# A copy moved ahead of a root, the last adds begun with the first tile, and the last tile cut at column 320, in a fused attention and gMLP kernel

## Chip, cores, metric

One core of a Trainium2 chip. The metric is the device time of one execution in microseconds; the profile's span is about 1.8 us shorter than it.

## The reference

A layer norm of x [2048, 512]; a dilated local attention on it (32 heads of 16, window 8, dilation 2, with output projection); a gMLP on it (projection to 2 x 688, gelu, layer norm of the second half, a [2048, 2048] product over tokens, gating, output projection); and the sum of x and both branches. Cut to what the change touches:

```python
x  = A_x
xn = layernorm(x)
return x + A_ref(xn, A_wqkv, A_wo) + B_ref(xn, B_w_in, B_w_sp, B_b_sp, B_w_out)

# A_ref: qkv = xn @ wqkv; softmax(q . k over 8 keys, 2 apart) @ v; @ wo
# B_ref: z = gelu(xn @ w_in); z1, z2 = halves; z2 = layernorm(z2)
#        (z1 * (w_sp @ z2 + b_sp)) @ w_out
```

## The kernel before

The tokens are 16 tiles of 128, in four blocks: tile `4 * tb + j` belongs to block j. `t0, i1, i2, i3` are the tiles of blocks 0 to 3. For every tile: statistics on VectorE, one over the root of the variance on ScalarE (`ln_root`), the norm applied on VectorE (`ln_apply`), and a transpose into `xnT`, from which TensorE makes q, k, v and z. A tile is transposed either on TensorE and copied out of PSUM by ScalarE (`tr`, `tr_copy`; for two tiles of block 0 half of the copy is VectorE's), or by a DMA that the SyncE queue issues (`tr_dma`). The engines run in the order in which the code emits instructions; waits come from the data.

```python
def ln_root(sl):
    A.activation(rstd[:, sl], mv[:, sl, 1], ACT.Abs_reciprocal_sqrt, bias=eps_t[:])

def tr_copy(i, pt, c0=0, c1=C):
    A.copy(xnT[:, c0:c1, i * P:(i + 1) * P], pt[:, c0:c1, :])

def tr_dma(i):
    j, tb = i % 4, i // 4
    SP.dma_start_transpose(xnT[:, :, i * P:(i + 1) * P], xall[:, j, tb, :])
...
    # end of the block 1 preparation; tiles 0 and 1 go over TensorE, 2 and 3 by DMA
    tr_dma(i1[2])
    ln_agg(i1[3])
    ln_root(col(i1[3]))
    ln_apply(i1[3])
    tr_dma(i1[3])
    load_x(SP, 3, 0, 4)
    pq3 = qk_tile()
    qk_part(pq3, 0, 3, 0, 4, (0,), kcs=range(2))
    pt = tr(i1[1])
    qk_part(pq3, 0, 3, 0, 4, (0,), kcs=range(2, 4))
    tr_copy(i1[1], pt)
    qk_part(pq3, 0, 3, 0, 4, (1,))
    qk_copy(pqs[2], 0, 2)
    qk_copy(pq3, 0, 3)
    for n in range(4):
        ln_stats(i2[n])
    ln_root(slice(2, 7, 4))
    ln_root(slice(10, 15, 4))
    for i in i2:
        ln_apply(i)
        tr_dma(i)
    for n in range(4):
        ln_stats(i3[n])
    ...                       # q and k of block 1: first from tiles 0 and 1, then from 2 and 3
    ln_root(blk_cols(3))
    qk_copy(pqs[0], 1, 3, 2, 4)
```

Then a fixed order of steps follows (`z j.tb`: z product of a tile; `zg`: its gelu, which frees the PSUM buffer; `q`: q/k product; `p`: products on VectorE). Three PSUM buffers of two banks take turns for z and q.

```python
ORDER = """
z2.0 z1.3 p1.1 z2.2 zg2.0 p0.1 zg1.3 q2.2 zg2.2 ...
... Or3 Oh3.0 Oh3.1 F3.0 F3.1 s3.0 s3.1 end
"""
LASTCUT = 288
```

The end of the program is the output projection of the last group, four tiles of 128 tokens, summed in PSUM. Tiles 0 and 1 share a buffer of two banks, tile 2 has its own, and tile 3 is split by columns over two buffers. Each sum is added to x by VectorE and stored.

```python
def out_half(o, h):                       # Oh: 5 matmuls for each of two tiles
    for tb in (2 * h, 2 * h + 1):
        for part in range(len(tiles["o", o][tb])):
            out_full(o, tb, part)

def last_adds():                          # end
    for tb, part, E in ((2, 0, SP), (3, 0, A), (3, 1, SP)):
        out_add(3, tb, part)
        out_store(3, tb, part, E)
```

Of the kernel before, what the change touches and what calls it, by code (L numbers as in the profile page):

```python
# [10 lines left out]
ALU = mybir.AluOpType  # L11
# [3 lines left out]
P = 128  # L15
# [11 lines left out]
F = 1376  # L27
FH = 688
FHALF = 344
MCH = 7  # L30
# [25 lines left out]
U10 Oh1.1 Fe1.0 U9 T8 Gi14 A43 Fe1.1 A44 T10 X13 A45 G11 s0.2 T9 A46 s0.3 F1.0 A47 A48 G13 F1.1 Gi11 s1.1 Xg13  # L56
U11 U12 Fe1.2 A49 T12 A50 A51 X14 A52 G15 Xg14 Fe1.3 U14 Gi13 F1.3 F1.2 A53 s1.2 T11 A54 T14 A55 O2 Gi15 s1.0
A56 U15 U13 T15 A57 Or2 xr2 Oh2.0 A58 A59 s1.3 Oh2.1 T13 Fe2.0 Fe2.1 xr3 F2.0 O3 Fe2.2 Fe2.3 F2.2 F2.1 s2.0
s2.2 F2.3 s2.1 s2.3 Or3 Oh3.0 Oh3.1 F3.0 F3.1 s3.0 s3.1 end
"""  # L60
NZ1 = 8
LASTCUT = 288


def slot_w(s):
# [4 lines left out]
def kernel(  # L70
# [13 lines left out]
    V = nc.vector  # L84
    A = nc.scalar
    G = nc.gpsimd
    PE = nc.tensor
    SP = nc.sync
# [19 lines left out]
    wout = r_w[:, 4096:4096 + MCH * D].rearrange("p (m n) -> p m n", m=MCH)  # L108
# [19 lines left out]
    uT = r_uz[:, NZ1 * FPAD:].rearrange("p (s m t) -> p s m t", s=2, m=MCH)  # L128
    pr_home = [r_pr[:, 0:8192], r_pr[:, 8192:16384], r_uz[:, (NZ1 + 8) * FPAD - 8192:]]
    pr = [h.rearrange("p (c w b t) -> p c w b t", w=4, c=C, b=TB) for h in pr_home]  # L130
    xl_t = [r_pr[:, n * D:(n + 1) * D] for n in range(4)]
    ol_t = [r_pr[:, (4 + n) * D:(5 + n) * D] for n in range(4)]
# [39 lines left out]
    def load_x(E, j, b0, b1):  # L172
        for tb in range(b0, b1):
            E.dma_start(xall[:, j, tb], xblk[j][:, tb])
# [42 lines left out]
    def ln_agg(i, parts=1):  # L217
        V.bn_aggr(mv[:, i, :], stats[:, i, 0:6 * parts])

    def ln_root(sl):  # L220
        A.activation(rstd[:, sl], mv[:, sl, 1], ACT.Abs_reciprocal_sqrt, bias=eps_t[:])

    def ln_apply(i):
        j, tb = i % 4, i // 4
        V.tensor_scalar(xall[:, j, tb, :], xall[:, j, tb, :], mv[:, i, 0:1], rstd[:, i:i + 1],
                        ALU.subtract, ALU.mult)
# [8 lines left out]
    def tr_copy(i, pt, c0=0, c1=C):  # L235
        A.copy(xnT[:, c0:c1, i * P:(i + 1) * P], pt[:, c0:c1, :])
# [12 lines left out]
# [3 lines that stand above are left out]
# [57 lines left out]
    def qk_part(pq, j, m, b0, b1, ccs=(0, 1), p0=None, kcs=range(C)):  # L309
        sd, c0 = m // 2, 2 * (m % 2)  # L310
        p0 = b0 if p0 is None else p0
        xv = xnT[:].rearrange("p k (b j t) -> p k b j t", b=TB, j=4)
        for cc in ccs:
            for kc in kcs:
                PE.matmul(pq[:, cc, p0 * P:(p0 + b1 - b0) * P], wqk[:, sd, kc, c0 + cc:D:C],  # L315
                          xv[:, kc, b0:b1, j, :], start=(kc == 0), stop=(kc == C - 1))
# [7 lines left out]
    def qk_copy(pq, j, m, b0=0, b1=TB, p0=None):  # L324
        sd, c0 = m // 2, 2 * (m % 2)
        p0 = b0 if p0 is None else p0
        if sd == 0:
            dst = qs[:, j, c0:c0 + 2, b0 * P:b1 * P].rearrange("p c (b t) -> p c b t", b=b1 - b0)
        else:
            dst = ks[:, c0:c0 + 2, HALO:HALO + S].rearrange("p c (b j t) -> p c b j t", b=TB, j=4)[:, :, b0:b1, j, :]  # L330
        cast = A.copy(dst, pq[:, :, p0 * P:(p0 + b1 - b0) * P].rearrange("p c (b t) -> p c b t", b=b1 - b0))  # L331
        if sd == 1:
            for i in k_reads[j]:
                tc.declare_no_dep(cast.ins, i, reason="other token columns of the same rows")
            k_casts[j].append(cast.ins)

    def qk_tile():
        return ps_mm.tile([P, 2, TBS], F32, name="pq", tag="mm")
# [157 lines left out]
    def out_heads(o):  # L496
# [13 lines left out]
        if last:  # L510
            cuts[3] = [(pos[3][:, 0:LASTCUT], slice(0, LASTCUT)), (pb[:, 0, 0:D - LASTCUT], slice(LASTCUT, D))]
        tiles["o", o] = cuts
# [19 lines left out]
    def out_add(o, tb, part=0):  # L532
        pc, cs = tiles["o", o][tb][part]
        if o == 3:
            V.tensor_tensor(ol_t[tb][:, cs], pc, xl_t[tb][:, cs], ALU.add)  # L535
        else:
            V.tensor_tensor(ot_t[tb], ot_t[tb], xr_t[tb], ALU.add)

    def out_store(o, tb, part=0, E=SP):
        i = 4 * tb + ORD[o]  # L540
        pc, cs = tiles["o", o][tb][part]
        E.dma_start(out2[i * P:(i + 1) * P, cs], (ol_t if o == 3 else ot_t)[tb][:, cs])

    def out_full(o, tb, part=0):
        pc, cs = tiles["o", o][tb][part]
        for m in range(MCH - 2):
            PE.matmul(pc, uT[:, o % 2, m, tb * P:(tb + 1) * P], wout[:, m, cs],  # L547
                      start=False, stop=(m == MCH - 3))

    def out_half(o, h):  # L550
        for tb in (2 * h, 2 * h + 1):
            for part in range(len(tiles["o", o][tb])):
                out_full(o, tb, part)

    def last_adds():
# [3 lines that stand above are left out]
# [4 lines left out]
    def blk(j):  # L563
        return [4 * tb + j for tb in range(TB)]

    def col(i):
        return slice(i, i + 1)
# [9 lines left out]
    t0, i1 = blk(0), blk(1)  # L577
# [50 lines left out]
    ln_apply(i1[2])  # L628
    tr_dma(i1[2])
    ln_agg(i1[3])  # L630
    ln_root(col(i1[3]))
    ln_apply(i1[3])
    tr_dma(i1[3])
    load_x(SP, 3, 0, 4)
    pq3 = qk_tile()
    qk_part(pq3, 0, 3, 0, 4, (0,), kcs=range(2))
    pt = tr(i1[1])
    qk_part(pq3, 0, 3, 0, 4, (0,), kcs=range(2, 4))
    tr_copy(i1[1], pt)
    qk_part(pq3, 0, 3, 0, 4, (1,))  # L640
    qk_copy(pqs[2], 0, 2)
    qk_copy(pq3, 0, 3)
# [41 lines left out]
    def halo_zero():  # L684
# [7 lines left out]
             "st": lambda k: st[k](), "N": z2_norm,  # L692
             "M": sm_max, "E": sm_exp, "S": lambda h, k: sm_sum(h, k), "R": sm_norm, "mask": add_mask,
             "G": g_mm, "Gi": g_bias, "U": u_mul, "T": u_tr, "A": lambda k: ap[k](),
             "O": out_heads, "Or": out_rest, "Oh": out_half, "Fe": out_evac, "F": out_add, "s": out_store, "end": last_adds,
             "halo": halo_zero, "wo": load_wo, "late": load_late, "xr": load_xr, "w": load_wsp}
    for tok in ORDER.split():
        name = tok.rstrip("0123456789.")
# [31 lines left out]
```

## Time and profile before

| | before |
|---|---|
| time, 3 runs | 202.38 us (202.26 to 202.41) |
| span of the profiled execution | 200.2 us |
| TensorE busy | 195.9 us, 98% |
| VectorE, ScalarE busy | 92%, 52% |
| transposes of block 1's second tile start | 12.91 us |
| first z load of block 2 | 21.67 us |
| last add ends | 197.83 us |

Busy shares say that TensorE is full; they don't say whether a hole of a tenth of a microsecond can be closed. That is read from single starts in the timeline. In the lines of the profile, PE is TensorE, PEld its weight loads, DVE VectorE, ACT ScalarE and SPq the queue of SyncE; a bracket gives the idle time before a group and what ended it. Two lines beside those that the prediction shows give the stretch that part 1 is about (start, duration, engine, line):

```profile
13.13 4.24 PE L315 MATMUL pq<-xnT,r_w 128*128 128x512 bf16 x30
17.20 1.04 PE L315 MATMUL pa<-xnT,r_w 128*128 128x256 bf16 x8
```

### The profile page before, as it was taken

The numbers are of one execution on the slowest core, as the hardware profiler recorded it, in microseconds if no ns is written. First come the engines' busy times: TensorE is split into PE (matmuls) and PEld (weight loads), VectorE is DVE, ScalarE is ACT, GpSimd is POOL, SyncE is SP. The second block draws the span as 40 slices with busy tenths as digits, with TensorE's granted clock in tenths as the row PEclk, the third lists the DMA queues.
The fourth block names the chain that finished last, engine by engine and source line by source line (L and its number), as shares of the span: only waits on it lengthen the run. The fifth ranks groups of instructions, "written<-read, shape, count | busy, mean of one in ns | idle before, by whom it ended". The sixth has DMA issues, their size and how long they took to land.

```text
span 200.2 us, 4094 instructions
## 1 busy us (share of the span) xinstructions
PE 195.9 (98%) x1691; PEld 124.1 (62%) x1691; DVE 184.5 (92%) x249; ACT 104.0 (52%) x176; POOL 18.5 (9%) x14
## 2 busy tenths in 40 slices
PE   7999999999999999999999999999999999999994
PEld 2869756665566666666656666666544646664562
DVE  5799999999989999999979999999999999999605
ACT  3586987899899986453431523708402230331400
POOL 3000000899400000000000000000000000000000
DMA  5877689940000095524467999199920295219863
GB/s 162 258 248 174 100 96 274 211 79 3 0 0 3 3 177 94 167 65 100 73 139 170 244 225 170 46 219 177 221 58 0 86 227 144 72 37 124 214 208 105
DMA packets 66562, 25.91 MB, mean 129 GB/s; under 512 B 56496, under 2 KB 66288, under 8 KB 66288
## 3 DMA queue, kind: packets, MB, share of 16 engines
q1 hardware_dynamic: 65824, 25.19, 57.8%
q10 hardware_dynamic: 720, 0.47, 0.7%
q8 instruction: 13, 0.21, 0.5%
q14 instruction: 5, 0.04, 0.1%
HBM read 10.13 MB, written 2.10 MB: 61 GB/s over the span
## 4 chain that ended last, share of the span: by engine, by line
PE 95%; DVE 2%; DMA 1%; issue 0%; SPq 0%; ACT 0%
PE pg L464 37%; PE pz L257 19%; PE pq L315 12%; PE pv L425 7%; PE po L547 7%; PE po L517 6%; PE pq L321 2%; DMA r_x<-in_A_x_dram 1%; PE pa L547 1%; PE pl L375 1%; DVE r_pr L535 1%; PE po L526 1%; PE pb L517 1%; PE pa L315 0%; PE pt L232 0%
## 5 line engine op out<-in xcount | busy, mean ns | idle before, releaser
L464 PE MATMUL pg<-z,r_qk 128*128 128x344 bf16 x448 | 66.8, 309 | 0.0
L464 PEld LDWEIGHTS <-r_qk 128*128 128x128 bf16 x448 | 43.8, 98 | 22.0 <-issue 0.4
L439 DVE TENSOR_TENSOR r_pr<-r_x,r_w 128x2048 bf16<-128x2048 bf16 x32 | 38.4, 1219 | 1.3 <-PE pl L375 1.0
L257 PE MATMUL pz<-w_z,xnT 128*128 128x344 bf16 x256 | 39.3, 309 | 0.0
L443 DVE TENSOR_TENSOR r_pr<-r_pr 128x2048 bf16<-128x2048 bf16 x28 | 33.9, 1218 | 0.4
L257 PEld LDWEIGHTS <-xnT 128*128 128x128 bf16 x256 | 24.9, 98 | 13.4 <-issue 0.4
L470 ACT ACTIVATE gs<-pg,b_col 128x688 bf16<-128x688 f32 x16 | 13.2, 833 | 35.4 <-PE pg L464 26.4
L355 DVE TENSOR_TENSOR r_pr<-r_qk 128x2048 bf16<-128x2048 bf16 x24 | 27.8, 1216 | 0.5 <-ACT r_qk L331 0.5
L315 PE MATMUL pq<-xnT,r_w 128*128 128x512 bf16 (+1 forms) x136 | 24.9, 335 | 0.0
L315 PEld LDWEIGHTS <-r_w 128*128 128x128 bf16 x144 | 15.9, 114 | 7.7 <-issue 0.6
L672 POOL CAST b_col<-b 128x16 f32<-128x16 bf16 x1 | 16.4, 16439 | 33.0 <-DMA b<-in_B_b_sp_dram 33.0
L530 ACT CAST r_qk<-po 128x512 bf16<-128x512 f32 x10 | 5.5, 588 | 22.7 <-PE po L547 22.7
L331 ACT CAST r_qk<-pq 128x1024 bf16<-128x1024 f32 (+1 forms) x16 | 15.4, 984 | 2.5 <-PE pq L315 2.4
L306 ACT ACTIVATE r_uz<-pz 128x688 bf16<-128x688 f32 x16 | 11.7, 740 | 6.6 <-PE pz L257 6.5
L517 PE MATMUL po<-r_lg,r_pr 32*128 32x512 bf16 x192 | 14.5, 375 | 0.0
L425 PE MATMUL pv<-xnT,r_w 128*32 128x512 bf16 x256 | 14.2, 379 | 0.0
L547 PEld LDWEIGHTS <-r_uz 128*128 128x128 bf16 x85 | 8.1, 98 | 9.4 <-issue 1.1
L364 DVE TENSOR_TENSOR r_pr<-r_pr 128x4096 bf16<-128x4096 bf16 x6 | 13.7, 2283 | 0.0
L547 PE MATMUL po<-r_w,r_uz 128*128 128x512 bf16 x60 | 13.6, 380 | 0.0
L281 ACT ACTIVATE junk<-z 128x688 bf16<-128x688 bf16 x16 | 12.4, 774 | 0.1
L275 ACT ACTIVATE z<-pz 128x688 bf16<-128x688 f32 x16 | 11.8, 740 | 1.2 <-PE pz L257 1.2
L425 PEld LDWEIGHTS <-r_w 128*32 128x32 bf16 x256 | 9.5, 138 | 4.2
(85 smaller groups left out, 194.6 us busy)
## 6 DMA issues: line engine op xcount, KB each, us to landing
r_lg<-in_A_wo_dram SPq DMA_DIRECT2D x8, 256.0 KB, 4.0
r_x<-in_A_x_dram SPq DMA_DIRECT2D x12, 128.0 KB, 3.2
out_dram<-r_qk SPq DMA_DIRECT2D x12, 128.0 KB, 2.2
r_w<-in_A_wqkv_dram SPq DMA_DIRECT2D x8, 128.0 KB, 3.5
r_qk<-in_A_x_dram SPq DMA_DIRECT2D x8, 128.0 KB, 2.2
w_z<-in_B_w_in_dram SPq DMA_DIRECT2D x4, 172.0 KB, 5.2
w_z<-in_B_w_in_dram SPq DMA_DIRECT2D x1, 688.0 KB, 5.4
r_w<-in_B_w_out_dram SPq DMA_DIRECT2D x1, 640.0 KB, 7.1
```

The source lines that it names most:

```text
L257: PE.matmul(pz[:, hh, 0:FHALF], xnT[:, kc, i * P:(i + 1) * P], wz[:, kc, hh * FHALF:(hh + 1) * FHALF], start=(kc == 0), stop=(kc == C - 1))
L315: PE.matmul(pq[:, cc, p0 * P:(p0 + b1 - b0) * P], wqk[:, sd, kc, c0 + cc:D:C], xv[:, kc, b0:b1, j, :], start=(kc == 0), stop=(kc == C - 1))
L331: cast = A.copy(dst, pq[:, :, p0 * P:(p0 + b1 - b0) * P].rearrange("p c (b t) -> p c b t", b=b1 - b0))
L355: prod = V.tensor_tensor(pr[g % 3][:, c].rearrange("p w b t -> p b w t"), q3.unsqueeze(2).broadcast_to([P, TB, 4, P]), k4, ALU.mult)
L364: V.tensor_tensor(pr[g % 3][:, 0:2], pr[g % 3][:, 0:2], pr[g % 3][:, 2:4], ALU.add)
L425: PE.matmul(pv[32 * tb:32 * tb + 32, dd, :], wv[:, kc, 2 * d2 + dd, :], xnT[:, kc, tb * TBS:(tb + 1) * TBS], start=(kc == 0), stop=(kc == ...
L439: V.tensor_tensor(pw_t[n], vp[:, :, off:off + P], a_sb[:, slot_w(w), ts].unsqueeze(1).broadcast_to([P, DH, P]), ALU.mult)
L443: V.tensor_tensor(pw_t[n] if dst is None else dst, pw_t[n], pw_t[m], ALU.add)
L464: PE.matmul(pg[:, hh, 0:FHALF], wsp[n][:, k, :], z2[:, k, hh * FHALF:(hh + 1) * FHALF], start=(k == 0), stop=(k == NT - 1))
L517: PE.matmul(pc, op[32 * tb:32 * tb + 32, d, o * P:(o + 1) * P], wo_r[32 * tb:32 * tb + 32, d, cs], start=(d == 8), stop=False, tile_positi ...
L547: PE.matmul(pc, uT[:, o % 2, m, tb * P:(tb + 1) * P], wout[:, m, cs], start=False, stop=(m == MCH - 3))
L672: G.tensor_copy(b_col[:], b16[:])
```

## The change

Its intent: close the hole that block 1's first q/k products leave by copying their tile before the root that has to wait for VectorE; let the last group's adds run tile by tile beside the matmuls; and make the very last add and store smaller.

```diff
--- before.py
+++ after.py
@@ -56,10 +56,10 @@
 U10 Oh1.1 Fe1.0 U9 T8 Gi14 A43 Fe1.1 A44 T10 X13 A45 G11 s0.2 T9 A46 s0.3 F1.0 A47 A48 G13 F1.1 Gi11 s1.1 Xg13
 U11 U12 Fe1.2 A49 T12 A50 A51 X14 A52 G15 Xg14 Fe1.3 U14 Gi13 F1.3 F1.2 A53 s1.2 T11 A54 T14 A55 O2 Gi15 s1.0
 A56 U15 U13 T15 A57 Or2 xr2 Oh2.0 A58 A59 s1.3 Oh2.1 T13 Fe2.0 Fe2.1 xr3 F2.0 O3 Fe2.2 Fe2.3 F2.2 F2.1 s2.0
-s2.2 F2.3 s2.1 s2.3 Or3 Oh3.0 Oh3.1 F3.0 F3.1 s3.0 s3.1 end
+s2.2 F2.3 s2.1 s2.3 Or3 Of Oh3.1 end
 """
 NZ1 = 8
-LASTCUT = 288
+LASTCUT = 320
 
 
 def slot_w(s):
@@ -532,7 +532,7 @@
     def out_add(o, tb, part=0):
         pc, cs = tiles["o", o][tb][part]
         if o == 3:
-            V.tensor_tensor(ol_t[tb][:, cs], pc, xl_t[tb][:, cs], ALU.add)
+            return V.tensor_tensor(ol_t[tb][:, cs], pc, xl_t[tb][:, cs], ALU.add)
         else:
             V.tensor_tensor(ot_t[tb], ot_t[tb], xr_t[tb], ALU.add)
 
@@ -544,8 +544,20 @@
     def out_full(o, tb, part=0):
         pc, cs = tiles["o", o][tb][part]
         for m in range(MCH - 2):
-            PE.matmul(pc, uT[:, o % 2, m, tb * P:(tb + 1) * P], wout[:, m, cs],
-                      start=False, stop=(m == MCH - 3))
+            mm = PE.matmul(pc, uT[:, o % 2, m, tb * P:(tb + 1) * P], wout[:, m, cs],
+                           start=False, stop=(m == MCH - 3))
+            if o == 3 and tb == 1:
+                tc.declare_no_dep(mm.ins, first_add[0], reason="other bank of the same buffer")
+
+    first_add = []
+
+    def out_first():
+        out_full(3, 0)
+        first_add.append(out_add(3, 0).ins)
+        out_store(3, 0)
+        out_full(3, 1)
+        out_add(3, 1)
+        out_store(3, 1)
 
     def out_half(o, h):
         for tb in (2 * h, 2 * h + 1):
@@ -628,15 +640,15 @@
     ln_apply(i1[2])
     tr_dma(i1[2])
     ln_agg(i1[3])
-    ln_root(col(i1[3]))
-    ln_apply(i1[3])
-    tr_dma(i1[3])
-    load_x(SP, 3, 0, 4)
     pq3 = qk_tile()
     qk_part(pq3, 0, 3, 0, 4, (0,), kcs=range(2))
     pt = tr(i1[1])
     qk_part(pq3, 0, 3, 0, 4, (0,), kcs=range(2, 4))
     tr_copy(i1[1], pt)
+    ln_root(col(i1[3]))
+    ln_apply(i1[3])
+    tr_dma(i1[3])
+    load_x(SP, 3, 0, 4)
     qk_part(pq3, 0, 3, 0, 4, (1,))
     qk_copy(pqs[2], 0, 2)
     qk_copy(pq3, 0, 3)
@@ -692,7 +704,7 @@
              "st": lambda k: st[k](), "N": z2_norm,
              "M": sm_max, "E": sm_exp, "S": lambda h, k: sm_sum(h, k), "R": sm_norm, "mask": add_mask,
              "G": g_mm, "Gi": g_bias, "U": u_mul, "T": u_tr, "A": lambda k: ap[k](),
-             "O": out_heads, "Or": out_rest, "Oh": out_half, "Fe": out_evac, "F": out_add, "s": out_store, "end": last_adds,
+             "O": out_heads, "Or": out_rest, "Oh": out_half, "Of": out_first, "Fe": out_evac, "F": out_add, "s": out_store, "end": last_adds,
              "halo": halo_zero, "wo": load_wo, "late": load_late, "xr": load_xr, "w": load_wsp}
     for tok in ORDER.split():
         name = tok.rstrip("0123456789.")
```

## The prediction

> **What bounds the kernel now.** I read the page first (engines, slices, chain that ended last), then the list of waits of the weight loads, then the timeline around 13 to 22 us, where the moved copy lies, and from 194 us on, where the adds lie, and last the chain there.
>
> ```profile
> PE 195.9 (98%) x1691; PEld 124.1 (62%) x1691; DVE 184.5 (92%) x249; ACT 104.0 (52%) x176; POOL 18.5 (9%) x14
> PE   7999999999999999999999999999999999999994
> PE 95%; DVE 2%; DMA 1%; issue 0%; SPq 0%; ACT 0%
> ```
>
> TensorE is never idle for a slice and carries 95% of the chain, so only two places can give time: short holes between its matmuls, and what follows its last matmul. The chain's pieces show where holes are. L257 is the z product (344 columns), L315 the q/k product. From 34.59 to 47.42 us the chain has 88 z matmuls in 12.83 us, 0.1458 us each: full rate. From 21.74 it has 24 in 3.61 us, 0.11 more than 24 x 0.1458 = 3.50. From 13.30 it has 30 q/k matmuls in 4.07 us: six of 512 columns at 0.2158 (24 take 5.18 us later on) and 24 of 256 columns at half that, 3.88 together, so 0.19 is lost. After 25 us I found no piece below full rate. These two holes, 0.30 us in sum, are all that the start can give.
>
> The first hole, in the timeline (start, duration, engine, line):
>
> ```profile
> 12.91 0.39 PE L232 MATMUL pt<-ident,r_x 128*128 128x128 bf16 x4
> 12.85 0.58 ACT L236 COPY xnT<-pt 128x512 bf16<-128x512 bf16 x1
> 13.69 0.30 ACT L221 ACTIVATE rstd<-mv,eps_t 128x1 f32<-128x1 f32 x1 [0.26 <-DVE mv L218]
> 13.89 0.56 ACT L236 COPY xnT<-pt 128x512 bf16<-128x512 bf16 x1
> 14.51 0.11 PEld L315 LDWEIGHTS <-r_w 128*128 128x128 bf16 x1 [0.18 <-issue]
> 14.36 1.93 ACT L331 CAST r_qk<-pq 128x1024 bf16<-128x1024 f32 x2
> ```
>
> The four transposes of block 1's second tile end at 13.30, but ScalarE waits for the aggregate of the fourth tile, does its root, and copies only at 13.89. Block 1's first matmul starts at 14.51; at full rate it would at 13.13 + 6 x 0.2158 = 14.43. Then two casts, back to back on ScalarE (ending 15.37 and 16.29), free the buffers of the next groups just as TensorE asks for them; that costs the rest of the 0.19.
>
> The second hole, in the waits and the timeline, eight microseconds later:
>
> ```profile
> PEld L257 <- DMA xnT<-r_x: 0.2, 1, 0.2
> 18.35 10.91 SPq L251 DMA_TRANSPOSE xnT<-r_x  x8
> 21.67 0.11 PEld L257 LDWEIGHTS <-xnT 128*128 128x128 bf16 x2 [0.20 <-DMA xnT<-r_x]
> ```
>
> The first z tile of block 2 waits for a DMA transpose issued at 18.35 that took 3.3 us to land, 21.65. This wait decides what the first part is worth.
>
> The tail, in the timeline of VectorE and the chain:
>
> ```profile
> 195.27 1.29 DVE L535 TENSOR_TENSOR r_pr<-po,r_pr 128x512 bf16<-128x512 f32 x2 [4.59 <-PE po L547]
> 196.47 1.05 DVE L535 TENSOR_TENSOR r_pr<-pa,r_pr 128x512 bf16<-128x512 f32 x2
> 196.76 0.64 PE L547 MATMUL pb<-r_w,r_uz 128*128 128x224 bf16 x5
> 197.44 0.39 DVE L535 TENSOR_TENSOR r_pr<-pb,r_pr 128x224 bf16<-128x224 f32 x1
> 196.47 1.36 DVE r_pr L535 x3
> ```
>
> The first tile's last matmul is over near 194.14 (worked out below), yet its add starts at 195.27, when the second tile's matmuls end: both share one buffer. From there the adds follow each other, and the chain names VectorE for the end. But TensorE itself ends at 196.76 + 0.64 = 197.40, and the last add starts at 197.44. So the queue of adds and the matmuls arrive together, and taking the queue away uncovers the matmuls at once.
>
> **What the Trainium skill says.** "TensorE: Matmul & The Clock Gate", section Back-to-back issue gap, gives N/2.4 + 2.5 ns between warm matmuls; for 512 columns 215.8 ns, and the trace has 215.8. "ScalarE: Activation LUTs", section What ACT_TABLE_LOAD costs, says consecutive ACTIVATEs overlap by about 93 ns; here the root ends 13.99 and the copy starts 13.89. "VectorE: DVE Perf Modes", section The TRN2 errata, gives (N+151)/0.96 ns for an fp32 tensor_tensor: 691 ns at 512 columns and 391 at 224; the trace has 680 to 691 and 391. "PSUM — Partial Sum Buffer", section PSUM bank collisions, says that two engines on different banks run clean: that is what lets the first add run beside the second tile's matmuls, and no run shows it yet.
>
> **The change, part by part.**
>
> Part 1, the copy ahead of the root. Nothing is added; the instruction order shows two copies in a row and then the root, on ScalarE only. The transposes end at 13.30 and the copy before ends at 13.43 with 0.09 overlap, so the copy runs about 13.35 to 13.91, 0.54 earlier. The root then starts at 13.82 instead of 13.69, 0.13 later. The casts start at 14.02 instead of 14.36, 0.34 earlier. TensorE loses nothing at 14.43, 15.29 and 16.15, and is 0.18 to 0.19 ahead at 17 us. Now the DMA: VectorE's apply of the fourth tile moves from 14.02 to 14.15 and ends at 14.56. The transposing DMA of that tile is issued at 15.00, held by the one before it on the SyncE queue (13.59 + 1.30), so the delay is hidden; the four loads after it (16.25 to 18.25) and the transpose at 18.35 stay. That one's input is applied by 17.96, or 18.09 after the change, still in time. It lands at 21.65 as before, and TensorE waits for it from about 21.39 instead of 21.58. The whole 0.19 is waited away: **0.00 us**.
>
> The 0.13 on VectorE is not hidden at once, for it runs without a gap from 14.3 to 22.1. The root of block 3 (22.14) and with it the first gelu (24.22, accumulator read over at 25.05) come 0.13 later, near 25.18. The q/k product that needs the buffer which that gelu frees starts at 25.18, paced by TensorE. With some 0.05 for the signal, TensorE loses between 0 and 0.06 there: **+0.03**. Later VectorE idles 0.53 at 57.24 for ScalarE, which absorbs the rest, and its pair sum for the first logits ends 1.0 us before TensorE takes it at 47.35.
>
> Part 2, adds from the first tile on. The count stays five. The first tile's five matmuls start at 192.90, so the last ends at 192.90 + 4 x 0.216 + 0.374 (the time of one) = 194.14, and the first add moves to 194.18, plainly beside matmuls; the second stays at 195.27, the third starts with its own matmuls' end, 195.07 + 4 x 0.216 + 0.374 = 196.31, + 0.04 = 196.35 instead of 196.47.
>
> Part 3, the cut at 320. TensorE's columns stay 512 in sum, so it ends at 197.39 to 197.40. The fourth add (320 columns, (320+151)/0.96 = 491 ns) is ready at 197.02 and not queued, ending 197.51; the fifth (192 columns, 357 ns) starts when TensorE ends, 197.43, and is over at 197.79 instead of 197.83. Gain 0.04. The last two stores then have the same bytes in all, and start almost as before, so the landing gains 0.02 to 0.06: **-0.04**.
>
> Sum: 202.38 + 0.00 + 0.03 - 0.04 = 202.37.
>
> **The rivals.** (a) The 0.19 gained at 14 us is kept. For it: TensorE is the chain from end to end. Against: the wait for the DMA at 21.67, whose issue does not move. It would need an earlier landing. Then 202.38 - 0.19 - 0.04 = 202.15. (b) The later root costs more: the fourth tile's transpose is late for block 1's second half (18.08; its landing does not show in the views), or gelu and casts push TensorE at 25 us and after. The delay is 0.13 at source, so up to +0.13: 202.5. (c) The tail gives more: the first two stores leave about 1.2 us and the third 0.12 us earlier, so the last two find free DMA engines, and the smaller last store lands faster. The last two landings took 1.7 and 1.5 us; with 0.1 off, 202.25. (d) The uncoupled first add collides with the second tile's matmuls or a wait is put there after all: the instruction order shows no new wait on TensorE, so I give it little.
>
> **Range and chances.** My sum is 202.37. I weight (a) with one in five (-0.04), and round to 202.33. The runs before span 0.15 us, and a rebuilt kernel may shift by as much again; (a) with (c) gives 202.1 and (b) 202.5. So 202.08 to 202.6. All the holes that I can name come to 0.3 us and the tail to 0.1, a fifth of a per cent; 2% is 4 us. Within 2%: 0.98; 0.01 either side.
>
> **What would show it.** Right: copy at 13.35, block 1's first matmul at 14.43, 24 matmuls there in 2.59 us; the wait of the z weight load for the DMA grows from 0.20 to about 0.39 and the load still starts at 21.67 +- 0.1; root of block 3 at 22.27; first add near 194.2, third at 196.35, and the chain naming TensorE up to 197.4 with only one add after it. Wrong: a z load before 21.5 (rival a, so the landing moved), the first q/k matmul after 25.3 or a new gap at 18 us (b), or a span that ends more than 0.1 us earlier against the last matmul (c).

## The result, and the profile after

The changed kernel took 202.09 us in the median of 6 runs (201.84 to 202.59), the kernel before 202.32 in 6 runs (201.94 to 202.56). The ratio is 0.9994, 95% interval 0.9978 to 1.0010: the same. Ratios are the mean time of one kernel's runs over that of the other's of the same rounds, so not quite the ratio of the medians quoted. Over the whole study the kernel before ran 42 times (mean 202.23) and the changed kernel 11 times (mean 202.24).

The timeline of the changed kernel, where the copy was moved:

```profile
12.93 1.07 ACT L236 COPY xnT<-pt 128x512 bf16<-128x512 bf16 x2
12.99 0.39 PE L232 MATMUL pt<-ident,r_x 128*128 128x128 bf16 x4
13.22 4.08 PE L315 MATMUL pq<-xnT,r_w 128*128 128x512 bf16 x30
13.90 0.30 ACT L221 ACTIVATE rstd<-mv,eps_t 128x1 f32<-128x1 f32 x1
14.10 1.92 ACT L331 CAST r_qk<-pq 128x1024 bf16<-128x1024 f32 x2
17.13 1.04 PE L315 MATMUL pa<-xnT,r_w 128*128 128x256 bf16 x8
```

Both copies now run as one piece and the root follows. TensorE's 30 matmuls take 4.08 instead of 4.24 us, and from the transposes to the next buffer it is 17.13 - 12.99 = 4.14 us, 0.15 less than before. So the hole was closed. What became of it stands in the same timeline 4 us later, and in the chain that ended last (start, us, what):

```profile
18.42 7.82 SPq L251 DMA_TRANSPOSE xnT<-r_x  x6
22.26 3.32 PEld L257 LDWEIGHTS <-xnT 128*128 128x128 bf16 x24 [0.86 <-DMA xnT<-r_x]
```

```profile
18.42 3.79 DMA xnT<-r_x
22.22 0.05 issue
22.26 3.67 PE pz L257 x24
25.94 5.18 PE pq L315 x24
```

The weight load of the first z product waits 0.86 us for the DMA transpose, 0.20 before. That is more than the gain: in this execution the transpose, issued 5.43 us after the transposes on TensorE as before (18.42 - 12.99; before 18.35 - 12.91 = 5.44), let TensorE go on after 3.84 instead of 3.32 us. The profiled execution of the changed kernel is therefore 0.6 us longer (span 200.8, time 202.59, the slowest of its six).

The tail of the changed kernel:

```profile
194.78 0.69 DVE L535 TENSOR_TENSOR r_pr<-po,r_pr 128x512 bf16<-128x512 f32 x1 [3.51 <-PE po L547]
195.86 0.69 DVE L535 TENSOR_TENSOR r_pr<-po,r_pr 128x512 bf16<-128x512 f32 x1 [0.39 <-PE po L547]
196.94 1.17 DVE L535 TENSOR_TENSOR r_pr<-pa,r_pr 128x512 bf16<-128x512 f32 x2 [0.39 <-PE pa L547]
197.42 0.58 PE L547 MATMUL pb<-r_w,r_uz 128*128 128x192 bf16 x5
198.03 0.36 DVE L535 TENSOR_TENSOR r_pr<-pb,r_pr 128x192 bf16<-128x192 f32 x1
```

Each add now waits for its own tile's matmuls (0.39 us idle before the second and the third), and the last starts 0.03 after TensorE ends at 197.42 + 0.58 = 198.00. From the first z load to the end of the last add it is 198.39 - 22.26 = 176.13 us, before 197.83 - 21.67 = 176.16. So 176 us of the program moved by 0.03 us; but for 0.02 us after the last add (column e below), everything else that differs between the two traces lies before the first z load.

### The profile page after: what moved, and what is told of

It is laid out like the page before. It is cut to its first block, busy times and chain, and to the rows that moved or that the text cites. A ratio compares the mean times of both kernels' runs of the same rounds, so it can differ in the third digit from the quotient of the medians. Undisturbed runs are those within 1.5% of the kernel's fastest.

```text
span 200.8 us, 4095 instructions
## 1 busy us (share of the span) xinstructions
PE 196.3 (98%) x1691; PEld 124.4 (62%) x1691; DVE 184.8 (92%) x249; ACT 104.1 (52%) x176; POOL 18.5 (9%) x14
## 4 chain that ended last, share of the span: by engine, by line
PE 91%; DVE 3%; DMA 2%; ACT 2%; issue 0%
PE pg L464 37%; PE pz L257 19%; PE pq L315 7%; PE pv L425 7%; PE po L547 7%; PE po L517 6%; PE pwm L586 2%; PE pa L547 2%; DMA xnT<-r_x 2%; DVE stats L211 1%; PE pq L321 1%; PE pl L375 1%; ACT r_qk L331 1%; PE po L526 1%; PE pb L517 1%; DVE r_x L225 0%
```

## The experiments

Twelve kernels ran, each timed in five rounds against the kernel before. One table holds what their profiles give. Times are differences between starts of one trace: **a** from the start of block 1's second tile's TensorE transposes to the first matmul of the fourth buffer (12.91 to 17.20 before); **b** from the issue of block 2's first DMA transpose to the first z load; **c** from those TensorE transposes to the first q/k product after the three z tiles; **d** from that product to the end of the last add; **e** from the last add's end to the end of the span, which is taken from the packed trace, because the views print the span to 0.1 us only. The first z load and the first z matmul below are the first weight load and the first matmul of the three z tiles.

| kernel | a | b | c | d | e | median us (runs) | ratio to before, 95% |
|---|---|---|---|---|---|---|---|
| before | 4.29 | 3.32 | 12.27 | 172.65 | 2.38 | 202.38 (3) | |
| after | 4.14 | 3.84 | 12.78 | 172.62 | 2.40 | 202.09 (6) | 0.9978 to 1.0010 |
| copy_only | 4.14 | 3.45 | 12.38 | 172.64 | 2.37 | 202.02 (5) | 0.9975 to 1.0001 |
| tail_only | 4.30 | 3.64 | 12.58 | 172.62 | 2.40 | 202.46 (6) | 1.0001 to 1.0028 |
| swap_before | 4.29 | - | 12.53 | 172.65 | 2.37 | 202.27 (6) | 0.9987 to 1.0014 |
| swap_after | 4.14 | - | 12.33 | 172.62 | 2.40 | 202.08 (6) | 0.9977 to 1.0004 |
| before_again | 4.30 | 3.78 | 12.71 | 172.64 | 2.38 | 202.13 (5) | 0.9980 to 1.0006 |
| after_again | 4.14 | 3.57 | 12.50 | 172.61 | 2.39 | 202.35 (5) | 0.9992 to 1.0018 |
| cut_only | 4.30 | 3.69 | 12.64 | 172.64 | 2.41 | 202.24 (5) | 0.9989 to 1.0014 |
| half_copy | 4.14 | 3.56 | 12.51 | 172.61 | 2.39 | 202.62 (5) | 1.0009 to 1.0038 |
| x3_before | 4.29 | - | 13.21 | 172.64 | 2.38 | 202.88 (5) | 1.0017 to 1.0043 |
| x3_half | 4.14 | - | 13.14 | 172.61 | 2.39 | 202.62 (6) | 1.0006 to 1.0030 |
| half_copy_swap | 4.13 | - | 12.20 | 172.61 | 2.40 | 201.84 (5) | 0.9972 to 0.9996 |
| adds_only | 4.30 | 3.41 | 12.35 | 172.65 | 2.37 | 202.17 (5) | 0.9989 to 1.0012 |

(A dash stands where another wait holds the first z load, or no wait shows.) My theory was that the gain at 14 us is waited away at block 2's DMA transpose; the rivals, that it is kept and hidden by noise, or that the later root gives it back.

### copy_only: part 1 alone

```diff
 # the kernel before, with these lines moved as in the change
-    ln_root(col(i1[3])); ln_apply(i1[3]); tr_dma(i1[3]); load_x(SP, 3, 0, 4)
     ...
     tr_copy(i1[1], pt)
+    ln_root(col(i1[3])); ln_apply(i1[3]); tr_dma(i1[3]); load_x(SP, 3, 0, 4)
```

> The kernel before with part 1 alone (copy of block 1's second tile ahead of the root of its fourth). Theory 1 (the gain at 14 us is waited away at the first z tile of block 2, whose DMA transpose lands when it lands): the 30 q/k matmuls after the transposes take 3.9 us in the chain instead of 4.07, block 1's first matmul starts 1.30 us after the first of those six 512-column ones (1.38 before); the z weight load's wait for the DMA grows by 0.19 over what the same landing would have given before; time within 0.1 us of before (202.3). Rival A (gain is kept): 0.18 us faster, z load 0.19 earlier. Rival B (the later root costs): up to 0.13 us slower, the first q/k product after the three z tiles late against the z tiles (more than 3.51 us after the first z load).

Its timeline:

```profile
13.04 4.08 PE L315 MATMUL pq<-xnT,r_w 128*128 128x512 bf16 x30
18.24 6.43 SPq L251 DMA_TRANSPOSE xnT<-r_x  x5
21.69 3.67 PE L257 MATMUL pz<-w_z,xnT 128*128 128x344 bf16 x24 [0.20 <-DMA xnT<-r_x]
```

The hole is closed (a = 4.14). The z product starts 3.45 us after the transpose's issue, between the values of kernels without the copy, and the issue is 5.42 after the TensorE transposes, where it was. The first q/k product follows the first z product by 3.51 us, as in the kernel before, so the later root costs nothing here. The times lie 0.2 us under those of before, though; the interval includes 1. The control below says how much that means.

### tail_only, cut_only, adds_only: the parts of the tail

```diff
 # tail_only: the change without the moved copy
 # cut_only:  the kernel before with
-LASTCUT = 288
+LASTCUT = 320
 # adds_only: tail_only with
-LASTCUT = 320
+LASTCUT = 288
```

> The kernel before with the adds from the first tile on and the cut at 320, without the copy. From the first matmul of the last five-matmul groups to the end of the last add: 4.93 us before, 4.90 after the change; this run should give 4.90. The time from the last add's end to the span's end, 2.38 before and 2.41 after the change, should be 2.3 to 2.45. Theory: the last matmul sets the end, so the time is 0.03 to 0.05 us under before, which the timing does not resolve. Rival C (earlier stores free the DMA engines): 0.1 us or more, and a shorter stretch from the last add to the end.

> The kernel before with the cut at 320 and nothing else: the adds still queue from the second tile's end. The fourth add then takes 0.49 instead of 0.45 us and the last can start only when that is over: from the first of the last five-matmul groups to the end of the last add 4.94 us (before 4.93, after the change 4.90): the longer fourth add eats what the shorter fifth gives. Time: within noise of before; if the tail part really costs 0.2 us through its smaller last store (384 bytes a row), it shows here, 202.45 or more.

> The kernel before with the adds from the first tile on, the cut left at 288. The last add has 224 columns and takes 0.39: from the first of the last five-matmul groups to its end 4.93 us less at most 0.01, because TensorE's own end sets its start; with the last store as in before, the stretch from the last add to the end is 2.36 to 2.37, not the 2.40 to 2.44 that three of four kernels with the cut at 320 and the early adds showed. So the tail is the same with either cut, and the time is that of before.

The column d settles the size. It is 172.64 or 172.65 in every kernel whose tail is that of before, in cut_only and in adds_only, and 172.61 or 172.62 in every kernel with both parts. The cut alone makes the fourth add longer by about what it takes from the fifth; here are the two adds of tile 2 and of the first part of tile 3, and the last add, in cut_only:

```profile
196.85 1.08 DVE L535 TENSOR_TENSOR r_pr<-pa,r_pr 128x512 bf16<-128x512 f32 x2
197.85 0.35 DVE L535 TENSOR_TENSOR r_pr<-pb,r_pr 128x192 bf16<-128x192 f32 x1
```

The pair takes 1.08 us instead of 1.05 and the last add waits for it. The early adds alone leave a last add of 224 columns behind TensorE's end. Together they give 0.03 us, the difference of 0.39 and 0.36 for the last add. Every kernel with the early adds returned correct outputs, so an add on one bank beside matmuls into the other bank of the same buffer did no harm in these runs.

What I expected of column e for adds_only held: with the last store as in before it is 2.37 (the larger figures in that expectation came from spans printed to 0.1 us). Column e follows the cut: 2.37 to 2.38 in the six kernels cut at 288 (mean 2.375), 2.39 to 2.41 in the eight cut at 320 (mean 2.397). The last store, of 192 instead of 224 columns, lands 1.53 to 1.56 us after its issue there, against 1.51 to 1.52. So the smaller last store does not land earlier but some 0.02 us later, and more than half of the 0.03 us is given back: d + e averages 175.024 us with the tail of before (five kernels) and 175.008 with both parts (seven). Why it lands later is not shown; with the cut at 320 the last two stores are also issued closer together (0.26 to 0.28 us apart, against 0.31 in the kernel before and 0.41 in adds_only). tail_only was timed 0.15% slower than before, which d + e cannot give.

### before_again, after_again: controls

The same two files once more.

> The kernel before once more, as a control. In the four runs so far the kernels with the copy lie at 202.0 to 202.2 and those without at 202.3 to 202.5, though the profiles show part 1 waited away and the tail 0.03 us shorter. If builds and loads of one kernel scatter by 0.2 us (start of the first loads, landing of the DMA transpose), this run lies anywhere within 0.3 us of the other runs of before. If the timing resolves 0.1 us, it lies within 0.1 us of them.

> The changed kernel once more, on the chip of its control. Waited away: within 0.1 us of before over many runs, and the stretch from the first z load of block 2 to the end of the last add is 176.13 again, 0.03 less than in before, wherever the landing lies. If the copy is worth 0.2 to 0.3 us and the tail costs 0.2, as the sums of the first runs read, it lies 0.1 under before and the two halves show again in the next two kernels.

The kernel before, built and loaded again, was timed at 202.13 beside 202.19 for its twin, and the changed kernel, 0.06% faster than before in its first session, was 0.05% slower in this one. So a difference of 0.2 us between two builds of this program, each of five or six runs, is not yet a difference between kernels: copy_only's -0.12% and tail_only's +0.15% lie near that size, and half_copy below shows the like once more. Why one build's runs stay together at one end of the range (copy_only 201.89 to 202.13, tail_only 202.29 to 202.70) I could not settle: only the first run of each has a trace in hand. What the traces do show is where two executions of one kernel differ: column b, 3.32 and 3.78 us in two executions of the kernel before, and 3.84 and 3.57 in two of the changed one, while d differs by 0.01 at most. With cut_only, adds_only and tail_only, b is 3.57 us on average over five executions without the copy and 3.61 over four with it. This is where the gain went: in all nine executions the first z load starts 0.04 to 0.05 us after the landing that the packed trace records, and the issue does not move with the copy. That the landing itself does not depend on the copy is as far as nine values spread over 0.5 us can tell; they could not show a dependence of 0.1 us. The times agree once several builds are taken: with the old order of z tiles and loads, the means of the four builds with the copy (202.18, 202.30, 202.00, 202.56) average 202.26, those of the five without it (202.25, 202.05, 202.50, 202.24, 202.20) 202.25.

One trap in reading: in cut_only the view of the timeline puts the first z product's wait down to a ScalarE cast, which ended at 22.01, 0.04 before it. In the kernel before the same cast ended at 21.99, after the z product had begun at 21.67, so it cannot be what is waited for; the DMA, 3.69 us after its issue, is.

### swap_before, swap_after: take the wait away

```diff
-z2.0 z1.3 p1.1 z2.2 zg2.0 p0.1 zg1.3 q2.2 ...
+z1.3 z2.0 p1.1 z2.2 zg1.3 p0.1 zg2.0 q2.2 ...
```

> The kernel before with the first two z2 tiles exchanged: the tile of block 1, long there, before the first tile of block 2, whose DMA transpose lands at 21.6 or later. If that landing holds TensorE, its wait (0.1 to 0.6 us by run) goes away: the first z load starts 0.09 earlier than the 21.67 of before, at full rate behind the q/k products, with no wait for the DMA. Behind it the first gelu becomes the wait: its accumulator is read at 25.05, and TensorE asks for the buffer at 25.08. So 0.1 us faster than a run of before with a 3.3 us landing, 0.3 or more against a run with a 3.8 us landing, and less scatter: all runs within 0.2 us of each other. If the landing does not set the end, time and scatter are as before (201.9 to 202.6).

> The changed kernel with the same exchange. TensorE then keeps the 0.19 us of part 1 as far as the first z load: it starts 0.27 earlier than in before (21.4 on before's clock). If the later root of the fourth tile matters, TensorE waits at the first q/k product after the three z tiles, for the gelu, which is 0.13 late (ready about 25.2 on before's clock): the stretch from the first z load to that product is 3.8 instead of 3.51 us, and the kernel is no faster than the one with the exchange alone, or 0.1 slower. If the delay of the root does not matter, it is 0.19 faster than the exchange alone.

The wait for the DMA is gone from both. In swap_before the first z matmul is at 21.58, 8.66 us after the transposes (8.76 before), in swap_after at 21.66, 8.51 after them: TensorE has kept the 0.15 us. But it isn't kept for long. This is the chain of swap_after (four pieces of `issue`, 0.01 to 0.04 us each, left out):

```profile
22.30 0.19 DVE mv L218
22.52 0.30 ACT rstd L221
22.82 0.47 ACT r_qk L331
23.30 1.28 ACT L275
24.60 0.84 ACT z L275 x2
25.48 5.34 PE pq L315 x24
```

VectorE's last statistics of block 3, the root, a cast, the load of the gelu table, and the first gelu, whose buffer the q/k product needs. From the first z matmul to that product it is 25.48 - 21.66 = 3.82 us, of which 3.51 are work. So behind the landing stands a second wait, and the root that the change made late (by 0.14 us against its aggregate: 13.90 in the profile after, where 13.76 would do) is part of it. In swap_before the second wait had another cause: the last x load of block 3 landed late (3.69 us after its issue), and VectorE with it.

### half_copy: the root not late

```diff
-    tr_copy(i1[1], pt)
+    tr_copy(i1[1], pt, 0, 2)
     ln_root(col(i1[3]))
+    tr_copy(i1[1], pt, 2, 4)
```

> The changed kernel with the copy in two halves, the root of the fourth tile between them: the root is not late, and the copy still ends by 14.3, before TensorE asks for it at 14.43. TensorE's 30 q/k matmuls keep the rate of the changed kernel (4.08 us in the timeline, 4.24 before), the root starts 0.03 after the aggregate, as in before. Waited away: still nothing in the time. Copy worth 0.2 to 0.3: as the copy alone with the tail, 202.1, or 0.13 better.

The profile did as expected: a = 4.14, the root at 13.62 against transposes at 12.84 (0.78 after them; 0.91 in the changed kernel, 0.78 before), and the z product where the DMA lands. The time did not: 202.62, 0.24% over before. Its profiled run took 202.06 and the other four 202.46 to 202.94. The only trace kept is that of the run of 202.06, so it can't account for the other four; with the controls I read them as the same unexplained scatter between loads of a program, but that is not shown.

### half_copy_swap: against both waits at once

> The changed kernel with the copy in two halves and block 1's z tile ahead of block 2's. With the late root the exchange gave 12.33 us from the transposes to the first q/k product after the z tiles, held by the gelu. The root in time should give 12.2, 0.13 less, unless the last x load is late, as in the exchange without the copy (12.53). Time 0.1 us under the exchange in the changed kernel, 201.9 to 202.1.

```profile
13.21 3.92 PE pq L315 x30
17.13 0.87 PE pa L315 x8
18.00 3.49 PE pq L315 x32
21.50 3.50 PE pz L257 x24
25.00 0.03 issue
25.03 5.34 PE pq L315 x24
```

Up to the z products TensorE has no hole: 30 matmuls in 3.92, 24 z matmuls in 3.50. Behind them the chain seems to have none either, but the records of matmuls that follow each other overlap (the last q/k record ends at 17.84 + 3.66 = 21.50 in the timeline, the first z record starts at 21.33), and that hides a short hole. The starts in the timeline show it:

```profile
21.33 3.66 PE L257 MATMUL pz<-w_z,xnT 128*128 128x344 bf16 x24
24.78 0.19 ACT L275 ACTIVATION_READ_ACCUMULATOR z<-pz 128x1 f32 x1
25.03 2.32 PE L315 MATMUL pq<-xnT,r_w 128*128 128x512 bf16 x10
```

From the first z matmul to the q/k product it is 25.03 - 21.33 = 3.70 us, and 3.51 where nothing waits. The product starts 0.06 us after the first gelu's accumulator is read (24.78 + 0.19 = 24.97). So 0.19 us of the second wait are left; the root in time took 0.13 of it away (c 12.33 in swap_after, 12.20 here, as expected). Only the wait for the landing is gone altogether.

The first q/k product comes 12.20 us after the transposes, the shortest of all kernels. The time is 201.84 us (201.69 to 202.13), 0.16% under before, and the interval (0.9972 to 0.9996) excludes 1. But half_copy's interval excluded 1 as well, on the other side, for a reason that was not found; so the time alone proves nothing. The profile's c, 0.07 to 0.58 us below all the kernels with the old order of z tiles and loads, is the better ground.

### x3_before, x3_half: an earlier landing by an earlier issue

```diff
     load_x(SP, 2, 0, 4)
+    load_x(SP, 3, 0, 4)          # and not after tr_dma(i1[3])
     for kc in range(C):
         SP.dma_start(w_z2[:, kc], B_w_in[kc * P:(kc + 1) * P, FH:F])
```

(x3_half is half_copy with this move.)

> The kernel before with the four loads of the last block's x ahead of the four loads of the z weights, so that nothing stands between block 1's and block 2's transposes on the SyncE queue. If the landing of block 2's first transpose holds TensorE: it is issued when its input is ready (some 5.15 us after the transposes of block 1's second tile, 5.43 before), with no load beside it, lands in 2.4 to 3 us, and TensorE does not wait for it: the first z load comes 8.67 us after those transposes (8.8 to 9.3 in the runs so far). The first q/k product then comes 12.2 to 12.3 after them, held by the gelu: 0.1 to 0.5 us faster than before by the run, with less scatter. Against: the z weights or block 1's own transposes land later among the earlier loads, and a wait shows at the second half of block 1 (5.17 us after the transposes in before).

> The same order of loads in the changed kernel, with its copy in two halves so that the root is not late. TensorE keeps the 0.17 us of part 1 as far as the first z load, 8.50 us after the transposes. If the gelu is the next wait, the first q/k product still comes 12.2 after them, as in the run without the copy: part 1 is worth nothing here either. If nothing else waits, it comes 12.02 after them and this kernel is 0.17 us faster than the one with the order of loads alone.

Both failed, in the way that the expectation named as the risk. x3_before in its timeline:

```profile
14.82 12.64 SPq L252 DMA_TRANSPOSE xnT<-r_x  x9
19.04 3.68 PE L316 MATMUL pq<-xnT,r_w 128*128 128x256 bf16 x32 [0.86 <-DMA xnT<-r_x]
22.56 3.66 PE L258 MATMUL pz<-w_z,xnT 128*128 128x344 bf16 x24
```

Block 1's own DMA transposes are issued at 14.82 instead of 13.59, since SyncE is busy with the loads till then, and TensorE waits 0.86 us for them at block 1's second half. At the z products no wait is left, but they start 9.71 us after the TensorE transposes, 8.76 in the kernel before. In x3_half part 1 is waited away here too: its wait is 0.94, and both kernels start the second half of block 1 6.11 to 6.19 us after the transposes, and the 0.08 between them is mostly in the issue of block 1's DMA transposes (1.97 us after those on TensorE in x3_before, 1.90 in x3_half), not the 0.15 of the copy. A gain upstream of a DMA-bound start is lost at whichever start that is.

## Why the prediction was right, point by point

- **Within 2%, 202.33 in 202.08 to 202.6** held: 202.09 in the median, 202.24 in the mean of 11 runs. That 202.09 lies just inside the range is luck: its lower end was set for rivals (a) and (c) together, which did not come, and the same kernel was timed at 202.35 when built again. What the mechanism says is no difference that the timing resolves, and that is what all 11 runs give.
- **Part 1 closes a hole of 0.18 to 0.19 us**: the mechanism held, the size is 0.15 to 0.17 (a: 4.29 or 4.30 without, 4.13 or 4.14 with). I had read 0.19 out of the chain's 4.07 us; the chain of half_copy_swap shows 3.92 for the same 30 matmuls without a hole, not my 3.88. A matmul of 256 columns takes 0.109 us there (32 in 3.49), a little more than half of the 0.2158 of 512.
- **All of it is waited away at the DMA transpose**: shown. The issue did not move (5.42 to 5.44 us after the TensorE transposes with and without), the load starts when the landing is there, and b is as large with the copy as without (3.61 and 3.57). With the landing out of the way, the 0.15 reaches the z products (8.66 and 8.51).
- **It lands at 21.65 as before, the wait grows to 0.39**: wrong as a number. The landing scatters over half a microsecond from run to run; the wait was 0.86, and the load started at 22.26, outside the 21.67 +- 0.1 that I had named as a sign. This was the largest term of all between two executions and I had none for it.
- **The later root costs +0.03**: the delay is there (0.14 predicted as 0.13), its cost is 0.00 in the three profiles with the late root and the old z order (after, copy_only, after_again), where the landing hides it (first z to q/k product 3.51 in each). It shows only when the landing is taken out of the way: 3.82 in swap_after, 3.70 with the root in time, about the 0.13 by which the root was late.
- **The tail, -0.04**: the last add ends 0.03 us earlier (0.04 predicted), because TensorE's end takes over at once, as said. The 0.02 to 0.06 for the landing of the last store have the wrong sign: with the cut at 320 the way from the last add to the end is 0.02 longer (column e).
- **Rival (a)**, the gain kept, and **(c)**, a better landing of the last stores, do not show in columns c and e of these traces; **(b)**, a wait at the second half of block 1, did not come with the change. **(d)** did not come.

## What to carry to other kernels

Before closing a hole on the bounding engine, walk on along that engine to the next start that a DMA decides and ask whether that DMA's issue moves; if it does not, the hole only moves there. Where several waits of nearly the same length stand behind each other (here the landing, then statistics, root, table load and gelu), work on them together and check between starts what is left: here each fix alone gave no time that the scatter let through, and the two together shortened the way to the q/k product to 12.20 us (12.27 to 12.71 in the five kernels without the copy and with the old order), with 0.19 us of the second wait still there. And when the effect is smaller than the scatter of one kernel with itself, compare stretches inside one trace rather than times; column d, 172 us long, repeats to 0.01 us among the kernels with the same tail.

## What the Trainium skill lacked or had wrong

- "TensorE: Matmul & The Clock Gate", Back-to-back issue gap, gives for a stream of weight load and matmul pairs in a real kernel about 131 ns at 512 columns and 81 ns at 128, and calls the formula N/2.4 + 2.5 ns the gap of a single isolated matmul. In this kernel every matmul has its own weight load, and the formula held in the stream: 215.8 ns at 512 columns (24 in 5.18 us), 145.8 at 344 (88 in 12.83 us), and 58 ns at 128 (24 in 1.40 us), where the formula gives 55.8.
- "DMA: Bandwidth & Descriptors", DMA Transpose (X-bar), has no time from issue to landing. Here one 128 x 512 bf16 transpose at the same place of the program let its reader go on 3.32 to 3.84 us after its issue in nine executions, and that spread was larger than any other difference between these nine traces from the transposes on.
- "PSUM — Partial Sum Buffer", PSUM bank collisions, says that two engines on different banks run clean. The runs agree (every output correct) and add what the page does not give, the speed: VectorE's add of 512 columns from one bank took 0.69 us beside matmuls into the other bank of the buffer and 0.68 to 0.69 in the kernel before, where the matmuls went to other buffers, and the ten matmuls kept their 2.33 us.
